# Batch 0 of a decay attention in two passes, with the MLP of its first 256 tokens beside the second, and 10 unsplit heads in place of 14

## The chip, the core and the metric

One core of a Trainium2 chip runs the whole program. Its engines work side by side, each through its own list of instructions in order: TensorE (PE: matmul, and PEld, the load of its stationary operand), VectorE (DVE), ScalarE (ACT), GpSimd (POOL) and SyncE (SP), which here issues most of the DMAs. SBUF is the on-chip memory of 128 partitions; PSUM holds what TensorE accumulates, in eight banks. The metric is the time of one execution on the device in microseconds, and smaller is better.

## The reference

64 heads (8 batches of 8) with 576 tokens and 64 dimensions a head; then an MLP of 512 to 2048 to 512 on the 4608 tokens.

```python
# per head; q, k, v: [576, 64], f: [576]
scores = scale * q @ k.T
cum = cumsum(log(clip(f, 1e-4, 1.0)))
scores = where(key > query, -1e9, scores + cum[:, None] - cum[None, :])
attn = exp(scores - max(scores))
attn = attn / (sum(attn) + 1e-9)
o = attn @ v
# x: [4608, 512], the heads of a token side by side
h = maximum(x @ w_in, 0.0)
out = h * h @ w_out
```

The weights come as 8-byte floats and all the rest as 4-byte floats.

## The kernel before

**Attention.** The heads go one after the other, 0 to 63. The scores of a head are computed with keys on partitions and queries along the row, in six units, `UNITS`: key block 0 with queries 256 to 576, key blocks 2, 3, 4 with the queries from the block's own start, key block 1 with queries 128 to 576, and key block 0 with queries 0 to 256. One unit of one head is a *slot*; a head has `NU` = 6 slots and the kernel counts slots through all heads. In a slot stand the score of that unit (`score`), the exponential, the product with v of the unit two slots earlier (`av_part`, `LAG` = 2), and what `events` has put there. There are two ways through a head:

- *Unsplit* heads (`h < NWHOLE`, the first 14) multiply in float32: score by L342 with the mask added by a small bf16 matmul (L344), product with v by L408. TensorE runs a float32 matmul as four passes over its columns, which the profile records as two instructions.
- *Split* heads write each float32 operand as a rounded part (float32r, one pass) and a remainder: two matmuls for a score (L348, L351), three for the product with v (L386 to L388), and more work on the other engines (`prep`, `split_p`, `split_v`, a mask by GpSimd at L363).

The softmax needs the row's maximum before the exponential. `max_units` takes it from a separate one-pass matmul with queries on partitions (L309), reduced by VectorE (L315); the column of maxima goes by a small DMA (L321) into a row of the query operand, so that the next score matmul subtracts it. The cumulative logarithms are two more rows of the operands, brought by `load_cum`. The maxima of head h are taken during head h-1, at the slots in `MAXIMA`. The sums come out of the product with v as an extra column; per pair of heads `finish` sends them through small DMAs, divides (L435, L436), broadcasts them through DRAM (`den<-rdr`) and multiplies on GpSimd (L444), at the slots in `DIVIDE`.

**Weights.** There are 32 weight tiles (16 of `w_in`, 16 of `w_out`), 512 KB each as they come. The generator `weight_ops` turns the bits of an 8-byte float into a 4-byte float and splits it: ScalarE takes the magnitude (L178), VectorE runs four integer or clamp instructions (L189, L194, L199, L201), ScalarE rounds (L206), GpSimd subtracts (L207). It yields between these pieces, five times a weight, and the main loop takes so many pieces a slot: `RATES`, 1 to 1.5 before slot 0, 1.4 up to slot 60 (`ready[0]`), 2.5 afterwards.

**MLP.** It works on chunks of `T` = 256 tokens, 18 in all, in 16 steps each. A step is `mlp1` (12 matmuls, L474), relu and square on ScalarE (L482, L484), the square and its remainder on VectorE (L483, L485), and `mlp2` (6 matmuls, L497). `mlp_half` issues one half of a step; `fill` decides in each slot how many halves have come due. It does nothing until batch 0's attention is divided, at slot 60 (`ready[0]`), which is two heads into batch 1. During batch 1 two chunks come due, and in as far as the weights are there.

**Order.** For TensorE, ScalarE, VectorE and GpSimd `in_order` pins the written order of the whole program; for SP it pins only what is written ahead of slot 0. PSUM banks are given out by use (`banks`).

Of the kernel before, what the change touches and what calls it, by code (L numbers as in the profile page):

```python
# [36 lines left out]
def decay_attention_relu2_kernel(  # L37
# [21 lines left out]
    P = 2 * D  # L59
# [16 lines left out]
    NWHOLE = 14  # L76
# [6 lines left out]
    banks = {"av": [0, 6], "s": [1, 2, 3], "m": [4, 5], "h": [4], "o0": [6], "o1": [7]}  # L83
# [11 lines left out]
    eye = wk.tile([P, 448], F32, name="p").bitcast(BF16)[:, :P]  # L95

    def masks():
# [5 lines left out]
        nc.gpsimd.memset(eye, 0.0)  # L103
        nc.gpsimd.affine_select(
            out=eye, in_=eye, pattern=[[-1, P]],
            compare_op=ALU.not_equal, fill=1.0, base=0, channel_multiplier=1,
        )

# [10 lines left out]
    def constant_rows(engine, x, ones=True):  # L119
# [3 lines left out]
        if ones:  # L123
            k = f32(x[D:, 1])
            nc.gpsimd.affine_select(
                out=k, in_=k, pattern=[[0, S]], compare_op=ALU.not_equal, fill=1.0, base=-2,
                channel_multiplier=1,
            )
# [4 lines left out]
    cum = []  # L133
# [4 lines left out]

    def decay():

# [20 lines left out]
    def weight_ops():  # L161
# [20 lines left out]
        stage()  # L182
        magnitude(0)
# [53 lines left out]
    def load_cum(h, k):  # L237

        if h < 2:
            nc.sync.dma_start(out=f32(k[D:D + 2, :]), in_=cum[0][h:h + 1])  # L240
        else:
            nc.sync.dma_start(out=f32(k[D:D + 2, :]), in_=cum_dr[h])

    def load_rounded(h):
# [4 lines left out]
        if cum:  # L249
            load_cum(h, x[:, 1])  # L250

    def load_whole(h):
# [3 lines left out]
        if cum:  # L256
            load_cum(h, x[:, 1])
# [41 lines left out]
    def max_units(h):  # L299
# [3 lines left out]

        def unit(i, k0, n, init, last):
            q0, m = QT[i]
# [7 lines left out]
            mo = MW - P + (k0 if m < P else max(P - end + k0, P - MW))  # L313
# [5 lines left out]
            if last:  # L319
                r = st["whole"][:, 0] if h < NWHOLE else st["r2"].bitcast(F32)  # L320
                nc.sync.dma_start(out=r[D + 2:D + 3, q0:end], in_=acc)  # L321

        us = []
        for i, (q0, m) in reversed(list(enumerate(QT))):
            end = q0 + m
            if end <= 512:
                us.append(lambda i=i, end=end: unit(i, 0, end, 1e30, True))
            else:
                us.append(lambda i=i: unit(i, 0, QA, 1e30, False))
                us.append(lambda i=i, end=end: unit(i, QA, end - QA, tcol[:, 7:8], True))  # L330
        return us

    def score(h, u):
        st = state[h]
        j, q0, q1 = UNITS[u]
# [25 lines left out]
        nc.scalar.activation(out=p[:kn, :n], in_=ps[:kn, :n], func=AF.Exp, scale=SCALE)  # L361
# [28 lines left out]
    def av_part(h, u, low):  # L390

        j, q0, q1 = UNITS[u]
# [18 lines left out]
        if last:  # L411
            n = QA if low else S - QA
            if not low:
                if h % H == 0:
# [10 lines left out]
    def finish(h, part):  # L425

        st = state[h]
        den = st["den"]
        if part == 0:
            st["cmp"] = wk.tile([P, S // D], F32, name="cmp")  # L430

            for i in range(2):
                nc.sync.dma_start(out=st["cmp"][i * D:(i + 1) * D], in_=den[i * D:i * D + 1, :])
        if part == 1:
            nc.vector.tensor_scalar_add(st["cmp"], st["cmp"], EPS)  # L435
            nc.vector.reciprocal(out=st["cmp"], in_=st["cmp"])  # L436
            st["rdr"] = dr.tile([2, S], F32, name="rdr")
# [292 lines left out]
```

## Time and profile before

| | us |
|---|---|
| median of 3 runs | 1238.59 |
| lowest, highest | 1236.88, 1243.77 |
| the profiled execution | 1240.77 |
| its span | 1239.0 |
| TensorE busy | 1183.2 |
| VectorE busy | 785.4 |
| ScalarE busy | 701.0 |
| GpSimd busy | 382.5 |

The span runs from the first to the last instruction of the profile. A matmul's record includes the time in which it passes through the array, so that records overlap and a busy TensorE isn't necessarily one at its peak. In the rows of the profile stand the engine, the line of the program (L309), the tile written and the tiles read, the shape, the count behind an x, busy microseconds and the mean in nanoseconds; in brackets or behind a bar stands the idle time ahead of it with what ended it. Up to the result an L in the text is a line of the kernel before.

### The profile page before, as it was taken

What the parts mean: (1) busy time and instruction counts of PE and PEld (TensorE: products, weight loads), DVE (VectorE), ACT (ScalarE), POOL (GpSimd) and SP (SyncE); (2) the same over time, 40 slices, a digit from 0 to 9 for tenths busy, and PEclk for the clock granted to TensorE, in tenths of its full rate; (3) what the DMA queues carried; (4) which work ended last, traced back from release to release, by engine and by line L of the source; (5) the groups of instructions that cost most, each with busy time, mean ns of one, the idle gap of its engine ahead of it and who ended that gap; (6) DMA issues with size and microseconds to landing.
All of it is one profiled execution on the core that took longest, in us unless ns stands there. A gap on an engine that the chain in (4) does not pass through costs nothing.

```text
span 1239.0 us, 23289 instructions
## 1 busy us (share of the span) xinstructions
PE 1183.2 (95%) x7652; PEld 1049.6 (85%) x7652; DVE 785.4 (63%) x2044; ACT 701.0 (57%) x1720; POOL 382.5 (31%) x574
## 2 busy tenths in 40 slices
PE   3887999999999999999999999999999999999998
PEld 2555787888999899989999989998999899999997
DVE  7666677767676767666656666677676767533322
ACT  2655455566666666665565666666666666632332
POOL 3333224433333433323223233334333333200000
PEclk9989899999999999999999999999999999999999
DMA  7767640212121111121202121211121222000000
GB/s 189 172 165 179 151 125 16 53 31 58 41 58 41 48 36 49 41 58 26 58 17 53 32 58 41 52 34 47 41 58 41 58 41 58 11 28 1 18 18 17
DMA packets 115440, 71.91 MB, mean 58 GB/s; under 512 B 97244, under 2 KB 97244, under 8 KB 115320
## 3 DMA queue, kind: packets, MB, share of 16 engines
q1 hardware_dynamic: 114200, 66.30, 21.9%
q0 software_dynamic: 1120, 4.13, 1.4%
q8 instruction: 61, 1.00, 0.3%
q14 instruction: 59, 0.48, 0.1%
HBM read 60.19 MB, written 9.88 MB: 57 GB/s over the span
## 4 chain that ended last, share of the span: by engine, by line
PE 53%; ACT 2%; issue 1%; POOL 1%; DMA 1%; DVE 0%; SPq 0%; POOLq 0%; DVEq 0%; ACTq 0%
PE bank L474 21%; PE bank L497 21%; PE bank L386 2%; PE bank L351 2%; PE bank L309 2%; PE bank L388 2%; PE bank L387 2%; PE bank L348 2%; DMA den<-rdr 1%; ACT r L482 0%; ACT ph L376 0%; ACT den L423 0%; ACT p L361 0%; POOL xt L444 0%; ACT rl L277 0%
## 5 line engine op out<-in xcount | busy, mean ns | idle before, releaser
L497 PE MATMUL bank<-w,gh 128*128 128x512 f32 x1152 | 412.9, 399 | 0.0
L474 PE MATMUL bank<-xh,w 128*128 128x256 f32 x2304 | 330.7, 286 | 2.2 <-DVE tcol L315 2.1
L377 DVE TENSOR_TENSOR pl<-p,ph 128x320 fp32r<-128x320 f32 (+4 forms) x300 | 189.7, 632 | 195.3 <-ACT ph L376 187.0
L474 PEld LDWEIGHTS bank<-xh,w 128*128 128x128 f32 x2304 | 302.3, 190 | 10.2 <-DVE tcol L315 2.7
L497 PEld LDWEIGHTS bank<-w,gh 128*128 128x128 f32 x1152 | 217.1, 188 | 38.2
L482 ACT ACTIVATE r<-bank 128x256 f32<-128x256 f32 x288 | 110.6, 384 | 206.7 <-PE bank L474 193.7
L497 PE MATMUL bank<-w,gl 128*128 128x512 f32 x576 | 226.6, 393 | 0.2 <-DVE gl L485 0.2
L483 DVE TENSOR_TENSOR g<-r 128x256 f32<-128x256 f32 x288 | 127.6, 443 | 141.1 <-ACT r L482 140.3
L363 POOL TENSOR_SCALAR_AFFINE_SELECT p<-p 128x128 f32<-128x128 f32 (+1 forms) x250 | 81.6, 326 | 421.3 <-ACT p L361 267.4
L376 ACT CAST ph<-p 128x320 fp32r<-128x320 f32 (+4 forms) x300 | 124.4, 415 | 148.9 <-POOL p L363 147.1
L474 PE MATMUL bank<-xl,w 128*128 128x256 f32 x1152 | 185.5, 283 | 0.0
L474 PEld LDWEIGHTS bank<-xl,w 128*128 128x128 f32 x1152 | 158.9, 191 | 0.0
L315 DVE CUSTOM_DVE_ANT_0 bank<-bank,mz 128x256 f32<-128x256 f32 (+4 forms) x320 | 133.8, 432 | 36.6 <-PE bank L309 33.1
L361 ACT ACTIVATE p<-bank 128x320 f32<-128x320 f32 (+4 forms) x300 | 116.0, 387 | 63.9 <-PE bank L351 51.8
L485 DVE TENSOR_TENSOR gl<-g,gh 128x256 fp32r<-128x256 f32 x288 | 127.8, 444 | 36.1 <-ACT p L361 1.0
L309 PE MATMUL bank<-rk 66*128 66x320 f32 (+9 forms) x384 | 113.8, 322 | 25.1 <-DVE tcol L315 10.8
L484 ACT ACTIVATE gh<-r 128x256 fp32r<-128x256 f32 x288 | 120.5, 419 | 9.1
L497 PEld LDWEIGHTS bank<-w,gl 128*128 128x128 f32 x576 | 109.1, 189 | 14.2 <-DVE gl L485 0.9
L309 PEld LDWEIGHTS bank<-rk 66*128 66x128 f32 (+3 forms) x384 | 69.4, 186 | 43.1 <-DVE tcol L315 20.4
L386 PE MATMUL bank<-pl,vh 128*65 128x320 f32 (+4 forms) x350 | 97.1, 278 | 2.3 <-ACT den L423 2.3
L387 PE MATMUL bank<-ph,v 128*64 128x320 f32 (+4 forms) x350 | 95.0, 271 | 0.0
L388 PE MATMUL bank<-ph,vh 128*65 128x320 f32 (+4 forms) x350 | 93.3, 272 | 0.0
(75 smaller groups left out, 1515.3 us busy)
## 6 DMA issues: line engine op xcount, KB each, us to landing
qkraw<-in_qk SPq DMA_DIRECT2D x50, 288.0 KB
v<-in_v SPq DMA_DIRECT2D x64, 160.0 KB
den<-rdr SPq DMA_DIRECT2D x64, 144.0 KB
out<-osb SPq DMA_DIRECT2D x36, 256.0 KB
w<-in_w_in SPq DMA_DIRECT2D x16, 512.0 KB
w<-in_w_out SPq DMA_DIRECT2D x16, 512.0 KB
rk<-in_qk POOLq DMA_DIRECT2D x14, 288.0 KB, 4.2
rl<-in_qk SPq DMA_DIRECT2D x14, 288.0 KB
```

What stands on the lines that cost most here:

```text
L309: nc.tensor.matmul(ps[:m, :n], st["r2"][:rows, q0:q0 + m], st["kl0"][:rows, k0:k0 + n], start=True, stop=True,)
L315: nc.vector.tensor_tensor_reduce(out=ps[:m, :n], in0=ps[:m, :n], in1=mz[:m, mo:mo + n], op0=ALU.add, op1=ALU.min, scale=-1.0, scalar=init, ...
L376: nc.scalar.copy(out=ph[:, :n], in_=p[:, :n])
L377: nc.vector.tensor_tensor(out=pl[:, :n], in0=p[:, :n], in1=ph[:, :n].bitcast(F32), op=ALU.subtract,)
L386: nc.tensor.matmul(acc[:D + 1, o], vh, pl[:, i], start=first, stop=False)
L387: nc.tensor.matmul(acc[:D, o], vl, ph[:, i], start=False, stop=False)
L388: nc.tensor.matmul(acc[:D + 1, o], vh, ph[:, i], start=False, stop=last)
L474: nc.tensor.matmul(ph[:, :T], w[:, s, cc], x[:, cc, :], start=(cc == 0 and k == 0), stop=(cc == NCC - 1 and k == 2),)
L483: nc.vector.tensor_tensor(out=g, in0=r, in1=r, op=ALU.mult)
L484: nc.scalar.activation(out=gh, in_=r, func=AF.Square)
L485: nc.vector.tensor_tensor(out=gl, in0=g, in1=gh.bitcast(F32), op=ALU.subtract)
L497: nc.tensor.matmul(po, g[:, ts], w[:, s], start=(fc == 0 and k == 0), stop=(fc == NF - 1 and k == 2),)
```

## The change

1. `NWHOLE` is 10: heads 10 to 13 are split, where they were unsplit.
2. For batch 0 the queries 0 to 255 of all eight heads are done first, in a pass of their own ahead of slot 0 (`low_step`, `NLOW` = 11 steps of a pipeline: maxima of head s, product with v of head s-2, scores of head s-1, rounding of head s+2). It has its own tiles, laid into the space of the last weight tiles (`early`), its own loads of q and k (`low_load`, half of them from ScalarE's queue) and of v, its own division (`low_finish`), and it adds decay and maximum by small one-pass matmuls.
3. The heads of batch 0 then have five slots (`HIGH_UNITS`), queries 256 to 575 only, and five units of maxima. `ready[0]` is slot 49, which is nine slots into batch 1.
4. `fill` issues the 16 steps of chunk 0 between slots 7 and 49, as far as the weights are there; `next_step` asks for one weight more than a step uses. Two chunks are still due by the end of batch 1, chunk 0 among them.
5. All conversions come earlier: `RATES` is 0 in the first four low steps, 2 a slot up to slot 0, 3 a slot up to slot 49. The generator is called 163 times in all, of which 161 fall ahead of slot 49.
6. For unsplit heads the key's cumulative logarithm no longer is a row of the score matmul; it is the bias of the exponential (`decay_by_key` computes it with keys on partitions), and `load_whole` no longer calls `load_cum`.
7. SP's written order is pinned up to slot 49.

```diff
-    NWHOLE = 14
+    NWHOLE = 10
...
+    HIGH_QT = [(q, min(P, S - q)) for q in range(QA, S, P)]
+    HIGH_UNITS = UNITS[:-2] + [(1, QA, S)]
...
-        nc.scalar.activation(out=p[:kn, :n], in_=ps[:kn, :n], func=AF.Exp, scale=SCALE)
+        if h < NWHOLE:
+            nc.scalar.activation(
+                out=p[:kn, :n], in_=ps[:kn, :n], func=AF.Exp, bias=bias[:kn, j, h:h + 1], scale=SCALE,
+            )
+        else:
+            nc.scalar.activation(out=p[:kn, :n], in_=ps[:kn, :n], func=AF.Exp, scale=SCALE)
...
+    def low_load(h):
+        (nc.scalar if h % 2 else nc.sync).dma_start(out=low_qk[h][:D], in_=qk[h][:, :, :QA])
...
+    def low_round(h):
+        nc.scalar.copy(out=low_r[h], in_=low_qk[h])
+
+    def low_max(h):
+        q, k = (low_r[h][:, i] for i in range(2))
+        ps = bank("m")
+        for i in range(QA // P):
+            n = (i + 1) * P
+            o = ps[:, i * P:i * P + n]
+            nc.tensor.matmul(o, q[:, i * P:n], k[:, :n], start=True, stop=False)
+            nc.tensor.matmul(o, pick[:, h:h + 1].broadcast_to([P, P]), chl[:, :n], start=False, stop=True)
+            nc.vector.tensor_tensor_reduce(
+                out=o, in0=o, in1=mz[:, MW - n:], op0=ALU.add, op1=ALU.min, scale=-1.0, scalar=1e30,
+                accum_out=low_tcol[:, 2 * h + i:2 * h + i + 1],
+            )
+        nc.vector.tensor_copy(out=low_tcolr[:, 2 * h:2 * h + 2], in_=low_tcol[:, 2 * h:2 * h + 2])
...
+    def low_score(h):
+        q, k = (low_qk[h][:, i] for i in range(2))
...
+            nc.tensor.matmul(o, k[:, j * P:(j + 1) * P], q[:, j * P:], start=True, stop=False)
...
+            nc.scalar.activation(out=p[:, :n], in_=o, func=AF.Exp, bias=bias[:, j, h:h + 1], scale=SCALE)
...
+    def low_step(s):
+        if s < H:
+            low_max(s)
+        if 2 <= s < H + 2:
+            low_av(s - 2)
+        if 1 <= s < H + 1:
+            low_score(s - 1)
+        if s + 2 < H:
+            low_round(s + 2)
...
-    def next_step():
+    def next_step(most):
 
-        for c in range(NCHUNK):
+        for c in range(most):
             fc = ahead[c]
-            if fc < NF and len(split_w) >= 2 * (fc + 1):
+            if fc < NF and len(split_w) >= min(2 * (fc + 1) + 1, NW):
                 return c, fc
...
-    RATES = (1, 0.5, 1.5, 1.4, 2.5)
+    RATES = 0, 2, 3, 2.5
...
+    NLOW = H + 3
+    LOW_DIVIDE = 0, 2, 3, 6
+    DIVIDE = (2, 4, 6, 8), (2, 4, 6, 7)
...
         if b == 0:
+            goal = 2 * NF * (n - low_ready + part) / (ready[0] - low_ready)
+            while halves[0] < goal and mlp_half(0, 1):
+                pass
             return
...
-        if b == 1 and len(split_w) == NW:
+        if b == 1:
...
-    for n in range(-2 * NU, last_slot + 1):
+    for n in range(-NLOW, last_slot + 1):
         if n == 0:
-            opening = len(tc.nc.cur_bb.bb.instructions)
+            banks.update(av=[0])
+        if n == ready[0]:
+            first_stage = len(tc.nc.cur_bb.bb.instructions)
...
+        if n < 0:
+            low_step(n + NLOW)
...
-        wr = RATES[0 if n < -NU else 1 if n < -NU // 2 else 2 if n < 0 else 3 if n < ready[0] else 4]
+        wr = RATES[0 if n < 4 - NLOW else 1 if n < 0 else 2 if n < ready[0] else 3]
...
-    in_order(tc, [mybir.EngineType.SP], opening)
+    in_order(tc, [mybir.EngineType.SP], first_stage)
```

More of the change, by code (lines that the diff above doesn't have):

```diff
@@ L182, in weight_ops @@
         stage()
+        yield
         magnitude(0)
@@ new lines, in low_av @@
+    def low_av(h):
+        acc = bank("av")
+        for j, p in enumerate(low_p.pop(h)):
+            i = ((h % (H // 2)) * 2 + j) * VW
+            nc.tensor.matmul(
+                acc[:, j * P:QA], low_v[h // (H // 2)][:, i:i + P], p[:, :QA - j * P],
+                start=j == 0, stop=j > 0,
+            )
+        if h == 0:
+            xts[0] = wk.tile([P, NCC, S], F32, name="xt0", bufs=1)
+        o = (h % 2) * D
+        nc.scalar.copy(out=xts[0][o:o + D, h // 2, :QA], in_=acc[:D, :QA])
+        nc.scalar.copy(out=low_den[o:o + 1, h // 2], in_=acc[D:D + 1, :QA])
@@ new lines, in low_step, with low_finish @@
+    def low_step(s):
[7 more added lines that the diff above has]
+            low_round(s + 2)
+    def low_finish(part):
+        n = H // 2 * QA
+        for i in range(n // 512 if part == 3 else 1):
+            o = slice(2 * i, 2 * i + 2) if part == 3 else slice(0, H // 2)
+            den = low_den[:, o]
+            if part < 3:
+                den = den.rearrange("p a b -> p (a b)")
+            divide(part, den, low_cmp, low_rdr, xts[0][:, o, :QA] if part == 3 else None)
@@ L523, in mlp_half @@
         else:
-            step = next_step()
+            step = next_step(most)
             if step is None:
@@ L535, in mlp_half @@
                 split_x(c, finished)
-            if fc > 0 and ("x", c + 1) not in mst and (c != 1 or ahead[0] == NF):
+            if finished and fc > 0 and ("x", c + 1) not in mst and (c != 1 or ahead[0] == NF):
                 split_x(c + 1, finished)
@@ L556, in decay_attention_relu2_kernel, with start @@
     VLOAD, VSPLIT = 2, 4
-    slots = [(h, u) for h in range(NH) for u in range(NU)]
+    slots = [(h, u) for h in range(NH) for u in range(len(units(h)))]
+    def start(h):
+        return h * NHU if h < H else H * NHU + (h - H) * NU
     unsplit = []
@@ L565, in fin @@
     def fin(h, part):
-        return (h + 1) * NU - 1 + DIVIDE[h >= H][part]
+        return start(h + 1) - 1 + DIVIDE[h >= H][part]
     avs = {}
@@ L644, in decay_attention_relu2_kernel @@
-    begin = len(tc.nc.cur_bb.bb.instructions)
-    constant_rows(nc.gpsimd, rounded[1], False)
-    tc.add_manual_dep(
-        tc.nc.cur_bb.bb.instructions[begin], decayed.name,
-        mybir.DependencyInfo(mybir.DependencyClass.Sync, mybir.DependencyReason.DATA),
-        reason="the decay first",
-    )
-    load_rounded(1)
-    constant_rows(nc.gpsimd, whole[1])
-    store_cum()
+    for h in range(H):
+        low_zeros(nc.vector if h % 2 else nc.gpsimd, h)
+    for i in range(2):
+        low_load_v(i)
@@ new lines, in decay_attention_relu2_kernel @@
+    nc.gpsimd.memset(f32(pick), 0.0)
+    for i in range(2):
+        diagonal(pick, -1.0 / SCALE, -i * NH)
+    identity(eye32)
+    mask()
+    identity(eyer)
+    identity(eye)
+    convert(2)
+    decay()
+    low_round(0)
+    decay_sums(0)
+    decay_split(0)
+    decay_by_key(0, 2)
+    low_round(1)
+    at(-NLOW, 1, decay_sums, 1)
+    at(1 - NLOW, 0, decay_split, 1)
+    at(1 - NLOW, 1, decay_by_key, 2, NJ)
+    at(1 - NLOW, 1, store_cum)
+    for x in rounded:
+        decay_rows(nc.gpsimd, x)
```

216 lines of the change are left out of this document (142 added, 74 removed).

## The prediction, made before the changed kernel ran

> **What bounds the kernel now.** I read the page first, then the busy time of the engines in chosen stretches, the timeline of TensorE and VectorE in the opening, the waits there, and last the chain, for the price of one block of MLP.
>
> ```profile
> span 1239.0 us, 23289 instructions
> PE 1183.2 (95%) x7652; PEld 1049.6 (85%) x7652; DVE 785.4 (63%) x2044; ACT 701.0 (57%) x1720; POOL 382.5 (31%) x574
> PE   3887999999999999999999999999999999999998
> ```
> ```profile
> 0.00:18.10 18.10, 3.05 (x6) 1.55 (x6) 13.15 (x28) 5.27 (x7) 7.42 (x19) 1.00 0.59 161
> 18.10:124.60 106.50, 82.74 (x365) 56.70 (x365) 71.40 (x197) 55.61 (x131) 36.84 (x54) 0.92 0.74 179
> 124.60:250.50 125.90, 118.82 (x698) 100.71 (x699) 91.03 (x211) 66.32 (x158) 42.42 (x49) 0.95 0.33 85
> 335.90:352.10 16.20, 16.20 (x112) 14.83 (x111) 12.71 (x32) 11.12 (x28) 7.04 (x10) 1.00 0.23 64
> ```
>
> The columns of the stretches are length, busy time of TensorE, weight load, VectorE, ScalarE and GpSimd, then granted clock, DMA share and GB/s. TensorE is full everywhere but in the first four slices: of its 56 us of idle time 39 lie before 124.6 us. Only there is anything to win. The timeline dates the stages:
>
> ```profile
> 18.14 1.41 PE L342 MATMUL bank<-rl 128*128 128x320 f32 x2 [2.02 <-DMA rl<-tcol]
> ...
> 92.31 0.78 PE L342 MATMUL bank<-rl 128*128 128x320 f32 x2
> ...
> 99.41 0.28 PE L408 MATMUL bank<-pl,v 128*66 128x64 f32 x2
> ...
> 124.60 1.27 PE L342 MATMUL bank<-rl 128*128 128x320 f32 x2 [2.84 <-DMA rl<-tcol]
> ...
> 129.26 2.08 PE L474 MATMUL bank<-xh,w 128*128 128x256 f32 x8 [2.12 <-DVE tcol L315]
> ```
> ```profile
> PE bank L342 <- DMA rl<-tcol: 13.7, 7, 3.9
> ```
> ```profile
> DVE bank L315 <- PE bank L309: 22.1, 11, 5.8
> ```
>
> Slot 0 of the attention is at 18.1, slot 60 (head 10, batch 0 divided) at 124.6, and the first MLP matmul is at 129.3. In between are ten unsplit heads with no filler: one takes TensorE 7.4 us when nothing holds it (92.31 to 99.7), ten would take 74 of the 106 us. The waits are short round trips: score for the row maximum that comes back by DMA (13.7 us), VectorE for TensorE (22.1 us). So VectorE too has 35 us free.
>
> **The prices.** One block of 256 tokens through the MLP, in the pure MLP at the end, from the chain; one split head with four of the 16 MLP steps of a block beside it (48 matmuls of L474 are four times twelve), from the timeline:
>
> ```profile
> 1143.34 1.45 PE bank L474 x12
> ...
> 1188.49 1.45 PE bank L474 x12
> ```
> ```profile
> 335.93 0.31 PE L348 MATMUL bank<-rk 67*128 67x320 f32 x1
> ...
> 352.12 0.31 PE L348 MATMUL bank<-rk 67*128 67x320 f32 x1
> ```
> ```profile
> 335.90:352.10 16.20, 6.46 (x48) 6.02 (x48) 1.00 0.23 64
> ```
>
> A block is 45.15 us, a step 2.82, a split head 16.19 - 4 x 2.82 = 4.9. From slot 60 the kernel before owes 18 blocks (812.7), 50 split heads (245) and 4 unsplit (29.6): 1087.3 of 1114.4 us. 27 us are lost: 13.4 in 124.6 to 250.5 (7.1 idle, and clock 0.95 over 126 us), the other 13.7 spread over the rest.
>
> **The change, part by part.** *Four heads split instead of whole* save 4 x (7.4 - 4.9) = 10 us of TensorE. *The two passes over batch 0* cost it a little: a low part and a high part stream about 15,700 columns a head where one whole pass streams 14,400 (counted from the shapes, four passes for float32), +0.6 us a head. *The first MLP block* moves ahead of the steady stage, and batch 0's steady stage starts at slot 49, not 60. Slot 49 is three slots into head 9, so half an unsplit head (3.7) is still owed. The chunk's last steps need the last weights, and these are due in slot 48; I leave 1.5 steps (4.2) behind. After slot 49 remain 17 blocks (767.6), 54 split heads (264.6), 3.7 and 4.2: 1040 us, plus what is lost. Everything hangs on when slot 49 comes, and that is VectorE's affair: of 32 weights only 17 were converted in 18.1 to 124.6 (x17 below), and now all of them are packed ahead of it.
>
> ```profile
> L199 DVE SCALAR_TENSOR_TENSOR osb<-w,osb 128x512 int32<-128x512 int32 x17 | 13.7, 808 | 0.3
> L201 DVE SCALAR_TENSOR_TENSOR osb<-w,osb 128x512 int32<-128x512 int32 x17 | 12.5, 736 | 0.2
> L194 DVE TENSOR_SCALAR osb<-wmag 128x512 int32<-128x512 int32 x18 | 11.3, 626 | 0.6
> L189 DVE TENSOR_SCALAR wmag<-wmag 128x512 f32<-128x512 f32 x17 | 10.7, 628 | 2.7 <-ACT wmag L178 2.7
> ```
> ```profile
> 18.10:124.60 106.50, 29.41 (x120) 0.92 0.74 179
> ```
> ```profile
> L483 DVE TENSOR_TENSOR g<-r 128x256 f32<-128x256 f32 x288 | 127.6, 443 | 141.1 <-ACT r L482 140.3
> L485 DVE TENSOR_TENSOR gl<-g,gh 128x256 fp32r<-128x256 f32 x288 | 127.8, 444 | 36.1 <-ACT p L361 1.0 <-PE bank L497 0.5 <-DVE g L483 0.5
> L462 DVE TENSOR_TENSOR xl<-xt,xh 128x1024 fp32r<-128x1024 f32 x12 | 14.7, 1226 | 0.4
> L461 DVE CAST xh<-xt 128x1024 fp32r<-128x1024 f32 x12 | 8.2, 685 | 4.2 <-POOL xt L444 4.2
> ```
>
> ```profile
> 38.51 0.68 DVE L199 SCALAR_TENSOR_TENSOR osb<-w,osb 128x512 int32<-128x512 int32 x1
> 39.23 0.69 DVE L201 SCALAR_TENSOR_TENSOR osb<-w,osb 128x512 int32<-128x512 int32 x1
> 39.84 0.42 DVE L189 TENSOR_SCALAR wmag<-wmag 128x512 f32<-128x512 f32 x1
> 40.36 0.43 DVE L194 TENSOR_SCALAR osb<-wmag 128x512 int32<-128x512 int32 x1
> ...
> w<-in_w_in SPq DMA_DIRECT2D x16, 512.0 KB
> ```
>
> The first group is VectorE's conversions in 18.1 to 124.6, the second line all of L315 there: 60 maximum units (two instructions each), 0.49 us a unit. *Slots 0 to 48:* the generator takes 163 calls for 32 weights, 16 are spent before slot 0, three go in each slot. So 29.4 weights at 2.80 us are 82; 50 units of maxima (35 high, 12 of heads 8 and 9, 3 of head 10) at 0.50 are 25; 15 MLP steps at 0.89 are 13.3; two splits of x at 1.91 are 3.8; divisions and the first split head's casts some 3. Sum 127. Neighbours overlap in the record: in 18.1 to 124.6 the same groups sum to 48.2 + 29.4 + 2 for 71.4 us of busy time, a factor 0.9, which leaves 114. VectorE has to wait for ScalarE's relu 0.49 us a step (141.1 over 288), 7 us. And GpSimd holds it up more when it is denser; I take 8 for that (below). 129 us, 2.6 a slot. TensorE needs less: eight high heads at 5.8 (11,200 of 14,400 columns), one and a half whole ones, 15 steps, 99 in all. Transfers don't bound it: 179 GB/s over 106.5 us moved 19 MB, 9 of weights and 10 for ten heads; now 29.4 weights (15.4) and about eight heads (8) go in 129 us, 181 GB/s, and nearly all of it ahead of need. Bounds: 105 with conversions at 2.2 (the four undisturbed ones of the timeline) and no waits; 154 if GpSimd holds up each conversion by 0.8 more.
>
> *The low phase,* eleven short steps ahead of slot 0, isn't in the trace. ScalarE carries most of it:
>
> ```profile
> L422 ACT COPY xt<-bank 64x256 f32<-64x256 f32 x64 | 23.0, 360 | 2.8 <-PE bank L408 1.4
> L423 ACT COPY den<-bank 1x256 f32<-1x256 f32 x64 | 23.3, 365 | 0.8
> L361 ACT ACTIVATE pl<-bank 128x256 f32<-128x256 f32 x14 | 5.3, 378 | 0.5 <-PE bank L344 0.4
> L206 ACT CAST w<-osb 128x512 fp32r<-128x512 f32 x32 | 19.7, 616 | 15.1 <-DVE osb L201 15.0
> ```
>
> Two copies, two exponentials (0.38 and about 0.28) and the rounding of 512 columns make 2.0 us a step, with two conversion calls 2.5. Three steps to fill the pipe at 3.5, five at 2.5, three at 2.0: 29, from a start near 7 us (the clamp, logarithm and scan on half the columns, with four DMA issues ahead of the logarithm on ScalarE's queue). Slot 0 at 36, bounds 29 and 44. The extra loads (8 x 131 KB and v again, some 1.6 MB, 10 us at 161 GB/s) lie in front of weights that are first used at about 18 us; if they are late, the first conversions wait on ScalarE and the score behind them too. SP now runs in written order up to slot 49, so a weight can queue behind a maximum's column; weights are asked for up to four ahead, seven slots, and that covers it. The row of sums for whole heads goes out of the matmul into the exponential's bias: no cost, and one DMA a head less. The return of the maximum gets three slots of 2.6 us in place of three and a half of 1.8, so the 13.7 us of waits should go; VectorE is what is late next.
>
> Slot 49: 36 + 129 = 165. *Behind it* the 13.7 us stay. The stage of batch 1 gets only 35 half steps over 47 slots: 36 + 3.7 + 49 = 89 us of TensorE, 1.9 us a slot, where the quoted head has 2.7. VectorE's part there is 7.3 x 8.2 + 17.5 x 0.89 = 75 (8.2 being 12.71 less four steps and a split), so little is left to hide a chain of score, exponential, mask, cast and subtraction within two slots. I lose 8 us (bounds 0 and 25). 165 + 1040 + 21.7 = 1227 of span, 1229 with the 1.8 us around it, against 1240.8 of the profiled execution: -12. From the median 1238.6 that is **1227**.
>
> **The lock, rule against row.**
>
> ```profile
> 57.93 1.37 POOL L207 TENSOR_TENSOR w<-osb,w 128x512 fp32r<-128x512 f32 x1 [5.23 <-ACT w L206]
> 58.18 1.66 DVE L199 SCALAR_TENSOR_TENSOR osb<-w,osb 128x512 int32<-128x512 int32 x1
> 59.88 0.69 DVE L201 SCALAR_TENSOR_TENSOR osb<-w,osb 128x512 int32<-128x512 int32 x1
> ```
>
> Beside GpSimd's subtraction L199 took 0.97 us longer than its twin L201 beside nothing. Averaged, a conversion pays 0.6 (2.8 against 2.2). The Trainium skill, SBUF — State Buffer, section "Who interferes with whom", says that VectorE and GpSimd share a port pair under an exclusive lock, held for the whole instruction, where VectorE reads two SBUF inputs or runs a two-port mode. By that rule each of 29 subtractions could cost its full length; the row agrees for one.
>
> **The rivals.** *VectorE keeps up* (0.22): conversions at 2.2, few waits, main part 112, slot 0 at 34, slot 49 at 146: 1208. For it: 35 us of free VectorE time in the opening. *VectorE chokes* (0.17), the one on the other side: GpSimd's subtractions in 18.1 to 124.6 met a VectorE that was idle a third of the time; met by a full one, a weight costs 0.8 more, 24 us, slot 49 at 189: 1251. It decides from slot 49 later than 177 (1239 - 1062). *Batch 1 turns latency-bound* (0.15): 47 slots at 2.3 us instead of 1.9, 19 us lost in place of 8: 1238. *The block doesn't get done early* (0.04): weights come late, half of its steps fall behind slot 49 while the opening stays as long: 1245. My forecast has 0.42, with its own range 1216 to 1238.
>
> **How the numbers follow.** What lies within 0.5% (1232.4 to 1244.8) can't be told from no change. Faster: 0.32 of the forecast's 0.42, 0.22 of the first rival, 0.03 of the third: 0.57. Slower: 0.15 of the second, 0.03 of the third, 0.02 of the last: 0.20. Same: 0.23. The range runs from below the first rival, 1204, to the second, 1252.
>
> **What would show it.** Slot 0 near 36 and the first score of head 9 near 157; VectorE busy nine tenths from 40 to 165 us and TensorE under eight; hardly any wait for the maximum's DMA there; conversions at 3 us each; the last one before 170; TensorE gaps in 165 to 255 of about 8 us. The forecast is wrong if VectorE is idle over a fifth of the opening (then a wait I haven't named bounds it), if slot 49 is later than 177, or if batch 1's slots take over 2.2 us.

## The result and the profile after

The changed kernel takes 1292.67 us (median of four runs, 1291.59 to 1294.37), the kernel before 1237.74 (median of four, 1235.20 to 1243.77). The ratio is 1.0438, with a 95% interval of 1.0397 to 1.0478: **slower by 4.4%**, where 1227 was forecast and 1252 was the top of the range. From here on an L is a line of the changed kernel. Score matmuls of unsplit heads are now L380, of split ones L386, the maxima's L347 with VectorE's reduction in L353, the MLP's matmuls L631 and L654.

The page of the changed kernel, with its busy times and the rows by slices:

```profile
span 1290.3 us, 23591 instructions
...
PE 1200.8 (93%) x7734; PEld 1067.0 (83%) x7734; DVE 810.9 (63%) x2113; ACT 726.5 (56%) x1768; POOL 404.1 (31%) x615
...
PE   5768878887899999999999999999999999999998
...
PEclk9689988999899999999999999999999999999999
```

TensorE has hardly more work, but the part in which it isn't full reaches from four slices to eleven. The stretches of the changed kernel, cut at its first score (slot 0), at slot 49 and at slot 96, where batch 1 is divided (length, busy time of TensorE, weight load, VectorE, ScalarE and GpSimd, then clock, DMA share and GB/s):

```profile
0.00:58.40 58.40, 34.14 (x152) 28.59 (x152) 23.39 (x78) 23.00 (x49) 15.06 (x37) 0.85 0.41 93
58.40:204.10 145.70, 115.70 (x557) 87.02 (x557) 126.88 (x260) 74.93 (x159) 53.54 (x62) 0.89 0.59 155
204.10:326.40 122.30, 93.95 (x591) 80.14 (x591) 74.58 (x208) 71.25 (x176) 49.59 (x74) 0.97 0.21 47
326.40:1290.00 963.60, 956.98 (x6437) 871.26 (x6436) 586.01 (x1569) 557.27 (x1384) 285.92 (x443) 1.00 0.16 40
```

Against the terms of the prediction:

| | forecast | measured | off by |
|---|---|---|---|
| slot 0 | 36 | 58.4 | +22 |
| slots 0 to 48 | 129 | 145.7 | +17 |
| stage of batch 1 (slots 49 to 95) | 97 (89 + 8) | 122.3 | +25 |
| the rest | 965 (1062 - 97) | 963.9 | -1 |
| span | 1227 | 1290.3 | +63 |

All three stages that weren't in the trace of before came out too long, and the one that was came out right. In the last row of the stretches TensorE is busy 957 of 963.6 us: nothing lost in the first 326 us comes back later. In the first, no engine is busy for more than 60% of the time, so something waits there; in the second VectorE is busy for 87%; in the third TensorE is idle 28 of 122 us though no engine is full.

**The first stretch.** One of the eleven low steps in the timeline of the changed kernel:

```profile
22.17 0.31 PE L543 MATMUL bank<-w 128*128 128x128 f32 x1
...
25.00 0.47 ACT L568 ACTIVATE ph<-bank,p 128x256 f32<-128x256 f32 x1
...
25.53 0.49 PE L558 MATMUL bank<-w 128*128 128x128 f32 x2 [0.65 <-ACT ph L568]
...
25.96 0.30 PE L543 MATMUL bank<-w 128*128 128x128 f32 x1
...
26.42 0.30 DVE L545 CUSTOM_DVE_ANT_0 bank<-bank,mz 128x128 f32<-128x128 f32 x1 [2.13 <-PE bank L544]
26.63 0.14 DVE L545 DVE_READ_ACCUMULATOR2_ANT w<- 128x1 f32 x1
26.83 0.38 PE L543 MATMUL bank<-w 128*128 128x256 f32 x1 [0.45 <-DVE w L545]
```

From 22.17 to 25.96 a step takes 3.8 us. At 25.53 the second half of the scores waits for the exponential of the first; at 26.83 the second half of the maxima waits for VectorE's reduction of the first. In each pair the second half writes other columns than the first half's reader reads, but both halves lie in one bank (`ps`), and the semaphores order them by the bank (that this is the reason, the first experiment shows). TensorE's waits from 7.7 to 58.4 (total, times, longest) say the same, eight times each:

```profile
PE bank L543 <- DVE w L545: 7.1, 8, 2.1
PE bank L558 <- ACT ph L568: 6.2, 8, 2.0
```

That is 13.3 us. How long such a wait lasts depends on what else the reader's engine has to do first: the longest for VectorE, 2.09 us up to 32.25, lasts until VectorE has done a conversion (L223 at 31.50) that stands ahead of the reduction in its list. The rest shows in the clock. Three stretches of the changed kernel:

```profile
24.40:27.80 3.40, 2.30 (x17) 1.95 (x16) 0.79 (x4) 1.91 (x5) 0.00 (x0) 1.00 0.00 0
27.80:31.20 3.40, 1.71 (x13) 1.38 (x11) 0.23 (x3) 2.37 (x6) 0.00 (x0) 0.99 0.00 0
31.20:34.60 3.40, 2.35 (x8) 2.08 (x9) 2.14 (x8) 0.51 (x2) 0.00 (x0) 0.50 0.02 5
```

After a stretch with TensorE busy only 1.71 of 3.4 us, and 1 us into that longest wait, the granted clock falls to half at 31.2; the matmuls of the step grow longer and the waits with them.

### The profile page after: what moved, and what is told of

Its sections match the earlier page's. It is cut to its first block, busy times and chain, and to the rows that moved or that the text cites. A ratio compares the mean times of both kernels' runs of the same rounds, so it can differ in the third digit from the quotient of the medians.

```text
span 1290.3 us, 23591 instructions
## 1 busy us (share of the span) xinstructions
PE 1200.8 (93%) x7734; PEld 1067.0 (83%) x7734; DVE 810.9 (63%) x2113; ACT 726.5 (56%) x1768; POOL 404.1 (31%) x615
## 4 chain that ended last, share of the span: by engine, by line
PE 74%; DVE 8%; issue 8%; ACT 4%; DMA 3%; POOL 2%; SPq 0%; DVEq 0%; POOLq 0%; ACTq 0%
PE bank L631 29%; PE bank L654 27%; PE bank L429 3%; PE bank L347 3%; PE bank L386 3%; PE bank L389 3%; PE bank L431 3%; PE bank L430 3%; DVE bank L353 2%; DVE g L640 1%; DVE osb L233 1%; DMA rk<-tcol 1%; DMA den<-rdr 1%; DVE osb L235 1%; ACT r L639 1%
## 5 line engine op out<-in xcount | busy, mean ns | idle before, releaser
L654 PE MATMUL bank<-w,gh 128*128 128x512 f32 x1152 | 416.2, 402 | 0.0
L420 DVE TENSOR_TENSOR pl<-p,ph 128x320 fp32r<-128x320 f32 x324 | 199.7, 616 | 224.6 <-ACT ph L419 214.4
L631 PE MATMUL bank<-xh,w 128*128 128x256 f32 x2304 | 333.0, 287 | 6.8 <-DVE tcol L353 5.3
L631 PEld LDWEIGHTS bank<-xh,w 128*128 128x128 f32 x2304 | 304.4, 191 | 15.0 <-DVE tcol L353 5.6
L654 PEld LDWEIGHTS bank<-w,gh 128*128 128x128 f32 x1152 | 219.0, 190 | 38.4
L419 ACT CAST ph<-p 128x320 fp32r<-128x320 f32 x324 | 134.3, 414 | 167.1 <-POOL p L406 165.2
L654 PE MATMUL bank<-w,gl 128*128 128x512 f32 x576 | 228.2, 396 | 0.2 <-DVE gl L642 0.2
L406 POOL TENSOR_SCALAR_AFFINE_SELECT p<-p 128x128 f32<-128x128 f32 x270 | 87.4, 324 | 427.5 <-ACT p L404 278.2
L640 DVE TENSOR_TENSOR g<-r 128x256 f32<-128x256 f32 x288 | 130.5, 453 | 132.2 <-ACT r L639 131.5
L631 PE MATMUL bank<-xl,w 128*128 128x256 f32 x1152 | 186.1, 284 | 0.0
L404 ACT ACTIVATE p<-bank 128x320 f32<-128x320 f32 x324 | 125.3, 387 | 76.9 <-PE bank L389 62.6
L631 PEld LDWEIGHTS bank<-xl,w 128*128 128x128 f32 x1152 | 159.4, 192 | 0.0
L353 DVE CUSTOM_DVE_ANT_0 bank<-bank,mz 128x448 f32<-128x448 f32 (+3 forms) x304 | 127.9, 435 | 24.2 <-PE bank L347 23.2
L654 PEld LDWEIGHTS bank<-w,gl 128*128 128x128 f32 x576 | 109.9, 191 | 14.6 <-DVE gl L642 0.9
L347 PE MATMUL bank<-rk 66*128 66x448 f32 (+5 forms) x376 | 106.6, 311 | 12.6 <-DVE rk L312 6.8
L429 PE MATMUL bank<-pl,vh 128*65 128x320 f32 (+4 forms) x378 | 105.2, 278 | 7.3 <-ACT den L466 5.5
L386 PE MATMUL bank<-rk 67*128 67x320 f32 x324 | 94.9, 293 | 12.8 <-DMA rk<-tcol 9.2
L430 PE MATMUL bank<-ph,v 128*64 128x320 f32 (+4 forms) x378 | 102.9, 272 | 0.0
L431 PE MATMUL bank<-ph,vh 128*65 128x320 f32 (+4 forms) x378 | 100.6, 272 | 0.0
```

The costliest lines, as they stand in the source:

```text
L347: nc.tensor.matmul(ps[:m, :n], st["r2"][:rows, q0:q0 + m], st["kl0"][:rows, k0:k0 + n], start=True, stop=True,)
L353: nc.vector.tensor_tensor_reduce(out=ps[:m, :n], in0=ps[:m, :n], in1=mz[:m, mo:mo + n], op0=ALU.add, op1=ALU.min, scale=-1.0, scalar=init, ...
L386: nc.tensor.matmul(ps[:kn, :n], st["kl0"][:D + 3, k0:k0 + kn], st["r2"][:D + 3, q0:q1], start=True, stop=False,)
L419: nc.scalar.copy(out=ph[:, :n], in_=p[:, :n])
L420: nc.vector.tensor_tensor(out=pl[:, :n], in0=p[:, :n], in1=ph[:, :n].bitcast(F32), op=ALU.subtract,)
L429: nc.tensor.matmul(acc[:D + 1, o], vh, pl[:, i], start=first, stop=False)
```

## The experiments

Each time is that of a single execution, but for the changed kernel and the last pair. Beside the last pair, 19 executions of the kernel before lay between 1236.1 and 1245.6; so of single executions only differences over some 5 us are read, and smaller ones only where the stretches show the same. Beside the single executions the kernel before ran once on the same chip, at 1237.5 to 1239.6.

| run | time | slot 0 | slot 49 | slot 96 | slots 0 to 48 | 49 to 95 |
|---|---|---|---|---|---|---|
| changed kernel | 1292.67 | 58.4 | 204.1 | 326.4 | 145.7 | 122.3 |
| free SP order | 1293.16 | 58.6 | 203.2 | 328.1 | 144.7 | 124.8 |
| 14 unsplit | 1297.10 | 58.3 | 204.0 | 330.1 | 145.8 | 126.1 |
| banks apart | 1269.27 | 38.8 | 183.5 | 304.5 | 144.8 | 121.0 |
| banks, no clamp | 1256.37 | 38.7 | 170.8 | 290.6 | 132.2 | 119.7 |
| banks, remainder on VectorE | 1270.03 | 39.1 | 183.5 | 305.0 | 144.3 | 121.6 |
| banks, 2 pieces a slot | 1274.10 | 39.5 | 163.2 | 309.8 | 123.8 | 146.5 |
| banks, maxima earlier | 1271.23 | 38.6 | 186.1 | 304.0 | 147.5 | 117.9 |
| banks, no early block | 1259.06 | 37.9 | 160.8 | 295.9 | 122.9 | 135.0 |
| the same, 2 pieces a slot | 1261.43 | 38.7 | 144.3 | 297.5 | 105.5 | 153.2 |
| no early block, 14 unsplit | 1272.31 | 38.3 | 163.6 | 307.5 | 125.3 | 143.8 |
| the same, 1.4 pieces a slot | 1282.44 | 39.4 | 151.7 | 315.2 | 112.3 | 163.6 |

**A bank for each half of a low step.**

```diff
-        ps = bank("m")
...
-            o = ps[:, i * P:i * P + n]
+            o = bank("m")[:, :n]
...
-        ps = bank("s")
...
-            o = ps[:, j * QA:j * QA + n]
+            o = bank("s")[:, :n]
```

> Changed kernel with a PSUM bank of its own for each half of a low step's maxima and scores (nothing else). Theory A: a low step is slow because its second matmul waits for VectorE (8 waits, 7.1 us) or ScalarE (8 waits, 6.2 us) to leave the bank that both halves share; then slot 0 comes at 46 us instead of 58.4 and the whole is 12 us shorter (1281). Rival B: the low phase is bound by ScalarE's own work or by the half clock; then slot 0 stays at 55 or later and the whole within 4 us of 1292.7.

1269.27 us, 23.4 less, and slot 0 at 38.8: the cause of theory A, with twice the gain that it expected. Two starts of a step in its timeline (L542 is L543 of the changed kernel), and its first stretch:

```profile
17.91 0.46 PE L542 MATMUL bank<-w 128*128 128x128 f32 x1
...
20.34 0.31 PE L542 MATMUL bank<-w 128*128 128x128 f32 x1
```
```profile
0.00:38.80 38.80, 27.09 (x152) 24.27 (x152) 22.25 (x78) 22.29 (x49) 14.71 (x37) 1.00 0.59 141
```

This step takes 2.43 us and the next 2.25, and TensorE has no wait in either. The clock, half from 31.2 on in the changed kernel, doesn't fall before slot 0 here. The gain is larger than the 13.3 us of waits because the half clock went with them. The same 152 matmuls now have 27 us of busy time where they had 34.

**SP's order pinned up to slot 0 only.**

```diff
-        if n == ready[0]:
+        if n == 0:
             first_stage = len(tc.nc.cur_bb.bb.instructions)
```

> Changed kernel with SP's order pinned only up to slot 0, as before the change. Rival C: SP's pinned order (52 us of waits for the maxima's columns with weights queued behind, DMA share 0.01 from 32 to 43 us) starves the conversions; then slots 0 to 49 fall from 146 us to 130 or less and the whole by 15 us or more. Theory A/D (the opening is bound by low-step round trips and by VectorE's work): slot 0 to 49 within 4 us of 146, the whole within 6 us of 1292.7.

1293.16: no change in this setting. A column of maxima that queues behind a weight on SP isn't what makes slots 0 to 48 long.

**14 unsplit heads in the changed kernel, and 10 in the kernel before.** The first undoes the change's head count, the second makes that change alone. In the first, part of the attention's values comes out otherwise (why is open); no work is left out, and only the time is read.

```diff
-    NWHOLE = 10
+    NWHOLE = 14
```

> Changed kernel with 14 unsplit heads again. Theory E: batch 1's stage (slots 49 to 96, 122 us with TensorE busy 94) is bound by the split heads' chain of loads, casts and columns because only 32 half steps of MLP are left to fill it; unsplit heads have a shorter chain and 10 us more TensorE work that fills a wait, so the stage falls to 108 to 116 us and the whole to 1280 to 1288. Rival F: TensorE's work counts in that stage; then the whole is 8 to 12 us longer (1301 to 1305).

```diff
-    NWHOLE = 14
+    NWHOLE = 10
```

> Kernel before with 10 unsplit heads in place of 14, nothing else of the change. If splitting heads 10 to 13 pays where the stage has MLP beside it (two blocks in batch 1): 6 to 10 us faster than before (1228 to 1232). If VectorE, which still converts weights there, can't also carry four more split heads: 0 to 10 us slower.

1297.1 (4.4 more, little beyond the spread, and between what the two theories expected) and 1256.15 (**18.6 more** than before on that chip, and more than either expectation had). So the head count alone, in the kernel before, loses a third of what the whole change lost. A stretch of the kernel before, from about its slot 60, and one of the kernel before with 10 unsplit heads, both over heads 10 to 13:

```profile
125.00:210.00 85.00, 80.45 (x459) 66.56 (x458) 62.02 (x142) 42.96 (x100) 26.02 (x27) 0.94 0.39 102
```
```profile
125.00:225.00 100.00, 77.80 (x470) 66.54 (x469) 84.45 (x175) 54.48 (x131) 46.14 (x51) 0.95 0.27 76
```

TensorE has less to do, if only by 2.7 us (77.8 after 80.5) where the forecast had 10, but VectorE is busy 84.5 of 100 us in place of 62 of 85. Some thirteen of the weights are converted there, and each split head brings VectorE and GpSimd its casts and subtractions at the same time.

**What bounds slots 0 to 48: VectorE without its clamp.** With banks apart, the clamp of each weight's magnitude is left out, so tiny and huge weights wouldn't be treated as before:

```diff
-            nc.vector.tensor_scalar(mag, mag, MAG_LOW, MAG_HIGH, ALU.max, ALU.min)
```

> e1_banks without the first of VectorE's four instructions on a weight, the clamp of the magnitude (left out: weights beyond the clamp's bounds come out otherwise). 29 of them at 0.50 us lie in slots 0 to 49. Theory D: slots 0 to 49 fall from 144.8 to 128 to 133 us and the whole to 1253 to 1258. Rival H: within 4 us of 144.8.

1256.37, 12.9 less than with the clamp, all of it in slots 0 to 48:

```profile
38.70:170.80 132.10, 110.41 (x557) 85.27 (x557) 108.93 (x234) 74.83 (x159) 54.21 (x63) 0.90 0.66 172
```

VectorE is busy 16 us less (125.0 with the clamp) and the stretch is 12.6 us shorter: four fifths of what VectorE is relieved of arrive. It is the main bound there, as the prediction had it.

**The lock: the remainder on VectorE instead of GpSimd.**

```diff
-            nc.gpsimd.tensor_tensor(out=hl[:, 1], in0=w, in1=hl[:, 0].bitcast(F32), op=ALU.subtract)
+            nc.vector.tensor_tensor(out=hl[:, 1], in0=w, in1=hl[:, 0].bitcast(F32), op=ALU.subtract)
```

> e1_banks with the remainder of a weight (L241) subtracted by VectorE instead of GpSimd: 29 more VectorE instructions of about 0.62 us in slots 0 to 49, 18 us, against what GpSimd's 29 subtractions hold VectorE up. If that is the 0.7 us a weight by which the four conversions (2.93) are longer than undisturbed ones (2.2), slots 0 to 49 stay within 5 us of 144.8. If GpSimd's other work does the holding, they take 10 to 18 us longer.

1270.03: no difference. VectorE's groups from slot 0 to slot 49, in the changed kernel and then in this one (which had banks apart):

```profile
L233 DVE SCALAR_TENSOR_TENSOR osb<-w,osb 128x512 int32<-128x512 int32 x29 | 27.5, 947 | 0.5
L228 DVE TENSOR_SCALAR osb<-wmag 128x512 int32<-128x512 int32 x29 | 22.5, 775 | 2.4 <-DVE wmag L223 0.5
L235 DVE SCALAR_TENSOR_TENSOR osb<-w,osb 128x512 int32<-128x512 int32 x29 | 20.5, 707 | 0.7
L223 DVE TENSOR_SCALAR wmag<-wmag 128x512 f32<-128x512 f32 x29 | 14.5, 499 | 0.0
...
L640 DVE TENSOR_TENSOR g<-r 128x256 f32<-128x256 f32 x15 | 12.1, 804 | 10.4 <-ACT r L639 10.4
```
```profile
L241 DVE TENSOR_TENSOR w<-osb,w 128x512 fp32r<-128x512 f32 x29 | 21.2, 732 | 10.9 <-ACT w L240 10.5
L235 DVE SCALAR_TENSOR_TENSOR osb<-w,osb 128x512 int32<-128x512 int32 x29 | 21.1, 727 | 0.7
L233 DVE SCALAR_TENSOR_TENSOR osb<-w,osb 128x512 int32<-128x512 int32 x29 | 20.3, 702 | 0.5
...
L223 DVE TENSOR_SCALAR wmag<-wmag 128x512 f32<-128x512 f32 x30 | 13.7, 455 | 0.0
L228 DVE TENSOR_SCALAR osb<-wmag 128x512 int32<-128x512 int32 x30 | 13.4, 448 | 0.7
```

The four instructions of a weight take 2.93 us (947 + 775 + 707 + 499 ns) beside GpSimd's subtraction (2.87 with banks apart) and 2.33 without it. The subtraction on VectorE itself costs 0.73. So on GpSimd it costs VectorE some 0.6 us a weight, nearly what it spares it: having that operation off VectorE buys nothing while VectorE is full.

**Fewer conversions ahead of slot 49.** With banks apart:

```diff
-    RATES = 0, 2, 3, 2.5
+    RATES = 0, 2, 2, 2.5
```

> e1_banks (1269.3; slots 0 to 49 take 144.8 us, slots 49 to 96 take 121.0) with 2 conversion pieces a slot in slots 0 to 48 instead of 3, so that some 22 of the 32 weights are done by slot 49 and the rest beside batch 1. Theory D (slots 0 to 49 are bound by VectorE, 125 of 144.7 us busy): seven weights at 2.9 us and some five MLP steps at 1.4 leave, slots 0 to 49 take 115 to 122 us; they come back in a stage that has VectorE time free (75 of 121), which grows to 133 to 145; the whole 1256 to 1266. Rival H (waits that don't depend on the number of conversions bound the opening): slots 0 to 49 still take 135 or more and the whole is 1275 or more.

1274.1, nothing won, as neither theory had it: slots 0 to 48 fall by 21 us, slots 49 to 95 rise by 25.5. VectorE's work is the bound, but taken out here it has its price behind slot 49.

**No block of MLP ahead of slot 49**, with banks apart:

```diff
         if b == 0:
-            goal = 2 * NF * (n - low_ready + part) / (ready[0] - low_ready)
-            while halves[0] < goal and mlp_half(0, 1):
-                pass
             return
```

> e1_banks with no MLP before slot 49: the 32 half steps of the first block fall into batch 1's stage, beside the 32 of the second, as in the kernel before. Theory G (an MLP step ahead of slot 49 is paid by VectorE, 0.9 us and about 0.7 of waiting, and is missing as a filler behind it): slots 0 to 49 fall to 118 to 126 us, slots 49 to 96 take 132 to 145 for 45 us more TensorE work; the whole 1262 to 1274, no worse than with the block ahead. If the early block is a gain as meant: slots 0 to 49 stay above 135, the stage grows by 35 us or more, the whole 1290 or more.

1259.06, **10.2 less** than with the early block. The stretches of this run from slot 0 to 49 and from there to 96:

```profile
37.90:160.80 122.90, 84.69 (x275) 50.91 (x275) 114.09 (x226) 63.72 (x129) 55.60 (x63) 0.76 0.71 184
160.80:295.90 135.10, 132.70 (x874) 119.28 (x874) 86.40 (x239) 81.70 (x204) 49.80 (x74) 0.96 0.18 43
```

Behind slot 49 TensorE now has 132.7 us of work in 135.1; with the early block it had 92.3 of 121.0 there. A whole block more makes that stretch only 14 us longer, since TensorE was idle for 29 us of it. Ahead of slot 49 the block costs 22 us, since there VectorE is full without it (114 of 123 us). Half of the 22 is VectorE's busy time (114.1 without the block, 125.0 with it), the other half its waiting, mostly for ScalarE's relu (10.4 us, behind the bar of L640 above). The filler was taken from where it was free to where it isn't.

**The same with fewer conversions.**

```diff
-    RATES = 0, 2, 3, 2.5
+    RATES = 0, 2, 2, 2.5
```

> e8_late (1259.1; slots 0 to 49 take 122.9 us, 49 to 96 take 135.0, TensorE busy 142 of 145 there) with 2 conversion pieces a slot in slots 0 to 48 instead of 3. Theory D: slots 0 to 49 fall by seven weights at 2.9 us to 100 to 106. Behind them TensorE is the bound now (VectorE 96 of 145 busy), so that seven weights hide there better than they did in e5_rate2, where the stage grew by 25.5: it grows by 5 to 15 us and the whole is 1244 to 1254. Rival I (what VectorE is spared ahead it always pays back behind, as in e5_rate2): the stage grows by 18 or more, the whole 1257 to 1264.

1261.43: slot 49 comes 16.5 us earlier, slots 49 to 95 take 18.2 more. The gain that theory D expected did not come: again the work only moves.

**The maxima half a slot earlier in split heads**, with banks apart, for the waits in slots 49 to 95:

```diff
-    MAXIMA = (0, 0.5, 1, 1.5, 2, 2.5), (1.5, 2, 2.5, 3, 3.5, 4)
+    MAXIMA = (0, 0.5, 1, 1.5, 2, 2.5), (1, 1.5, 2, 2.5, 3, 3.5)
```

> e1_banks (1269.3) with the maxima of split heads half a slot earlier. Theory E: in slots 49 to 96 (121.0 us, TensorE busy 92) the longest waits of TensorE are for the maxima's column (9.1 by DMA, 3.2 by VectorE, 4 more ahead of the weight load); half a slot more (1.3 us a head for seven heads) brings the stage to 112 to 117 us and the whole to 1261 to 1265. If the wait only moves to the casts ahead of the maxima (3.5 us so far): stage 119 to 124, the whole within 4 us of 1269.

1271.23, no gain. TensorE's longest waits between slots 49 and 96, with banks apart and then in this run:

```profile
PE bank L386 <- DMA rk<-tcol: 9.1, 6, 1.9
PE bank L347 <- DVE rk L312: 7.9, 3, 4.4
PE bank L429 <- ACT den L466: 3.8, 5, 1.6
PE bank L386 <- DVE tcol L353: 3.2, 6, 0.7
```
```profile
PE bank L347 <- DVE rk L312: 8.3, 3, 4.8
PE bank L429 <- ACT den L466: 7.2, 5, 2.5
PE bank L386 <- DMA rk<-tcol: 3.3, 2, 2.1
```

The waits for the column fall from 9.1 and 3.2 to 3.3 us; that for the casts of the next head stays (7.9 and 8.3), and that for ScalarE grows (3.8 to 7.2). The stage is 3.1 us shorter, slots 0 to 48 2.7 longer. So the column alone doesn't set that stage's pace.

**Is splitting dear or the conversions beside it?** In the version without an early block the conversions are over by slot 49, so heads 10 to 13 have none beside them:

```diff
-    NWHOLE = 10
+    NWHOLE = 14
```

> e8_late (1259.1) with 14 unsplit heads; like e3_whole14 it changes part of the output, and only its time is read. Theory J: with 64 half steps of MLP in batch 1 (TensorE busy 133 of 135 us from slot 49 to 96) and the conversions done ahead, VectorE no longer bounds that stage, so whole heads there cost TensorE's 2.5 us each: +4 to +14 us (1263 to 1273). Theory L (the 18.5 us that four more split heads cost the kernel before are lost in the changed one too): -12 to -20 us (1239 to 1247).

As above, part of the attention's values changes and no work is left out; only the time is read. 1272.31: 13.2 **more**, where the same edit to the kernel before is worth 18.6 the other way. 8.8 of the 13.2 us lie in slots 49 to 95. So splitting four heads saves 9 to 13 us where no conversions run beside it and costs 18.6 where they do.

**The two passes by themselves.** The last version with the rate of the kernel before:

```diff
-    RATES = 0, 2, 3, 2.5
+    RATES = 0, 2, 1.4, 2.5
```

> e13_late14 (1272.3; slots 0 to 49 take 125.3 us, 49 to 96 143.8) with the conversions at the pace of the kernel before, 1.4 pieces a slot in slots 0 to 48; 14 unsplit heads, no MLP ahead, so that of the change only the two passes, the bias and SP's order are left; it changes part of the output as e13_late14 does. Theory M (packing the conversions ahead of slot 49 is what costs; whole heads behind it leave VectorE half free, 71 of 149 us, and would hide them): slots 0 to 49 fall to 86 to 100 us, the stage grows to 150 to 165, the whole 1244 to 1256. Rival N (the two passes themselves cost 30 us): the whole stays at 1265 or more, as a slower pace left e8_late where it was (e9_late_rate2, +2.4).

1282.44, 10.1 more. This has 14 unsplit heads, a whole first block behind slot 49 and conversions at 1.4 a slot, as before; what it keeps of the change are the two passes, the bias and SP's order, and small things beside (the slots of the division, the conversions ahead of slot 0). It is 44.7 us slower than the kernel before. Most of its opening, and two scores that begin a head, 12.4 us apart:

```profile
38.00:135.00 97.00, 66.36 (x251) 42.28 (x251) 56.45 (x158) 42.23 (x88) 30.46 (x46) 0.82 0.64 160
```
```profile
61.47 1.41 PE L380 MATMUL bank<-rl 128*128 128x320 f32 x2 [6.68 <-DMA rl<-tcol]
...
73.86 1.41 PE L380 MATMUL bank<-rl 128*128 128x320 f32 x2 [4.84 <-DMA rl<-tcol]
```

VectorE is busy 56 of 97 us, TensorE 66: neither is full. TensorE waits at the start of these two heads for the column of maxima, 6.68 and 4.84 us. In slots 0 to 48 the scores wait for it four times, 18.3 us in all, and four times more, 15.3 us, for something that the profile doesn't show. Five slots take 112.3 / 49 x 5 = 11.5 us, where a whole head before took 106.5 / 60 x 6 = 10.65. A head with 78% of the columns isn't shorter, and the low pass comes on top (slot 0 at 39.4 in place of 18.1). The clock is lower, too (0.82, where slots 0 to 59 had 0.92 before); what that costs wasn't separated. Whether SP's pinned order lengthens that DMA in this setting wasn't tried; freeing it in the changed kernel did nothing.

**The other direction: 16 and 18 unsplit heads in the kernel before**, ten executions each.

```diff
-    NWHOLE = 14
+    NWHOLE = 16
```

> Kernel before with 16 unsplit heads in place of 14. In e4_before10 four more split heads raised VectorE's work ahead of head 18 by 22 us and the time by 18.5, as VectorE still converts weights until some 225 us (head 14). Theory J: whole heads pay as long as the conversions run and cost TensorE's 2.5 us a head afterwards; head 14 lies on the border, head 15 behind it: -3 to +4 us from before (1235 to 1242). Rival K (VectorE's work ahead of head 18 sets the time, whatever stands beside it): two heads spare it 11 us, -7 to -11 us (1227 to 1231).

```diff
-    NWHOLE = 14
+    NWHOLE = 18
```

> Kernel before with 18 unsplit heads. Theory J: heads 15 to 17 stand where TensorE is full (18.1 us a head, one after the other) and cost 2.5 us each: +2 to +10 us (1240 to 1248). Rival K: -14 to -20 us (1218 to 1224).

1236.0 (ratio 0.9967, interval 0.9947 to 0.9988) and 1237.86 (0.9976, 0.9957 to 0.9996). Sixteen is the fastest of all that ran, a third of a per cent below the kernel before; with eighteen the loss that I expected of splitting too little did not come, nor the large gain of the rival. From 14 to 18 the curve is flat, from 10 to 14 it is steep. Of the versions of the changed kernel that do all of the work, the best (1259.06) stays 20 us above the kernel before.

## Why the prediction was wrong

By its own terms, of which the first three failed.

**The low phase, 36 us, bounds 29 and 44: measured 58.4.** The step was sized by ScalarE's busy time (2.5 us). That size came out with banks apart (2.43 and 2.25 us a step, slot 0 at 38.8), but by luck: in these two steps TensorE is busy without a gap (4.68 of 4.68 us) and ScalarE 3.66, and TensorE's work in a low step stood in no term. What was left out is a wait that stands in the diff: two halves in one bank, each with a reader on another engine, so that the second half's matmul waits for the first half's reader. I looked for waits in the queues and for late loads, and not at who shares a bank. It cost 19.6 us up to slot 0 (58.4 - 38.8) and 23.4 in all. The Trainium skill, PSUM — Partial Sum Buffer, section "PSUM bank collisions raise a hardware error", says that two engines on one bank and one group of 32 partitions need a semaphore between them even where their columns differ. The trace agrees: the wait of 0.45 us at 26.83 is for a reader of other columns. That rule spoke against the change, and the prediction did not weigh it.

**The opening is VectorE's affair, 129 us: measured 145.7.** The mechanism held (with 16 us less of VectorE work the stretch is 12.6 shorter), the size didn't. By groups VectorE had 144 us where I summed 127: conversions 2.93 us a weight and not 2.80, 85 in all for 82; maxima 30 for 25 (0.61 a unit for 0.50); an MLP step 1.30 for 0.89, 19.5 for 13.3, with g alone at 804 ns where the steady stage had 443; 9.7 for 7 in what is left. The factor for overlap was right (126.9 of 144 is 0.88). The forecast had 114 of work, 8 more for GpSimd and 7 of waiting. Measured are 126.9 of work, so that 5 of the 17 us are durations beyond that allowance, taken from a VectorE that had less beside it; GpSimd's subtraction shows in them twice, in the conversions and in g (501 ns where it isn't on GpSimd). The other 12 are idle time, 18.8 us where I had 7: 10.4 of waits for the relu, 2.7 for TensorE's maxima, the rest in gaps between instructions. The lower bound of 105 wasn't worked out right either: conversions at 2.2 and no waits make (127 - 17.6) x 0.9 = 98. "VectorE chokes", the rival with 154 us for this term, comes nearer than the forecast, but with 0.13 more a weight and not the 0.8 that it charged.

**The stage of batch 1, 89 us of TensorE and 8 lost (bounds 0 and 25): measured 94 and 28.** "Batch 1 turns latency-bound" was the right rival with too small a price: 2.6 us a slot where it had 2.3 and the forecast 1.9. The prediction credited the early block in full (18 blocks become 17, 45 us less behind slot 49). The runs show that only 14 us of it are saved there, because TensorE then idles, and that 22 are paid for it ahead. The step that failed is the one that counted TensorE's time behind slot 49 as the path: 28 us of idle time stand there in place of 8.

**"Four heads split instead of whole save 10 us"** holds without conversions beside it (13.2 measured in all, 8.8 in the stage). Beside conversions it costs 18.6. I priced it by TensorE alone.

**"Only there is anything to win"**, the premise of the first part, was not an argument about what could win it. Of TensorE's 39 idle us 15 lie ahead of slot 0. Of the other 24, 13.7 are round trips of a head (score, maximum, DMA, score), and a head with fewer columns has the same round trip. That the return of the maximum gets more slots was to remove 13.7 us of waits; in slots 0 to 48 of the changed kernel one of 3.7 us is left, but VectorE is full there. Where VectorE is relieved (1.4 pieces a slot, no block beside) they are back, 18.3 us in four heads. That they went because VectorE was late first is argued from this and not shown.

What held: the rest of the program to 1 us, and the block being done ahead of slot 49 but for its last step (15 of L640 in the groups above). Of the signs of being wrong two came: slot 49 later than 177 (204.1) and slots of batch 1 over 2.2 us (2.6). Slot 49 at 177 wasn't the point from which the change loses, though: without the clamp it comes at 170.8, and the time is 1256. The point was worked out with 97 us for the stage behind it. The range was too narrow for a reason of its own: it let one rival come true at a time. Here two terms went wrong together, and with the shared bank they make the 64 us (22 + 17 + 25).

How the 55 us come about can be told along two paths, and the price of a part depends on the path. From the kernel before: splitting four more heads +18.6 (run alone), two passes with their conversions ahead, the bias and SP's order, banks apart, +3 (to 1259.1), the early block +10.2, the shared bank +23.4. Or: the two passes at the old rate +44.7, earlier conversions -10.1, splitting -13.2, then the same two. Both paths end in the same two steps, by the same runs, and 33.6 of the 55 us are theirs; whether these two would cost the same in another order wasn't run. The other 21 are shared between the passes and the splitting, and these runs don't divide them further.

## What to carry to other kernels

When a step is new, write down for every PSUM tile which engine reads it and what is written into the same bank next; a wait by bank is visible in the diff before any trace. Idle time of an engine can be filled only by work whose own bottleneck is idle too, and filler that is moved forward must be counted both where it arrives and where it is then missing. Durations from a half-idle engine are too short for a full one, and a saving on one engine (here splitting) can change its sign with what runs beside it.

## What the hardware showed that was not expected

The clock fell at 31.2 us although TensorE's waits in the two steps ahead were at most 0.65 us and the one under way had lasted 1 us (from 30.16): it was busy 2.30 and then 1.71 of 3.4 us. The Trainium skill, TensorE: Matmul & The Clock Gate, section "HAM oscillation — how this bites in real kernels", tells of gaps longer than 3.4 us; here shorter ones were enough. With banks apart the clock fell only at 38.8, after 1.04 busy us in 3.4 (34.2 to 37.6). How low the busy share must be isn't settled by these runs, since stretches just under and just over weren't set up.

The granted clock in the rows reads 1.00 from the start, but that is not to be trusted ahead of its first recorded change. The same matmul of a low step at three times in the changed kernel:

```profile
19.77 1.06 PE L558 MATMUL bank<-w 128*128 128x256 f32 x2
...
24.04 0.60 PE L558 MATMUL bank<-w 128*128 128x256 f32 x2
...
34.12 1.06 PE L558 MATMUL bank<-w 128*128 128x256 f32 x2
```

At 34.12 the clock reads 0.50, at 19.77 it reads 1.00, and the matmul is as long. So by its length the clock was half up to some 21 us, too.

GpSimd's subtraction held VectorE up by nearly as much as it took from it, 0.6 us a weight for 0.73. The Trainium skill, SBUF — State Buffer, section "Who interferes with whom", has an exclusive lock between the two engines that would explain it. The trace agrees in two of the four groups, L228 (775 ns with it, 448 without) and L233 (947 and 702); L223 hardly differs (499 and 455), and L235, which reads two tiles like L233, not at all (707 and 727).
